# Attention's chunks 4 to 15 in 64x64 tiles on all array quarters, with the sign bit of the weights taken by 16-bit words

## The chip, the cores and the metric

The kernel runs on one core of one Trainium2 chip. The metric is the device time in microseconds of one execution.

## What is computed

A linear attention with decay, and two MLPs behind it. In short, from the reference:

```
gamma = 1.0 - 2.0 ** (-5.0 - arange(H))
for t in range(S):
    state = gamma * state + einsum('bhd,bhe->bhde', k[:, :, t], v[:, :, t])
    y[:, :, t] = einsum('bhd,bhde->bhe', q[:, :, t], state) / sqrt(D)
x = y as (tokens, heads * D)
h = x @ moe_w_in;   x = (h * sigmoid(1.702 * h)) @ moe_w_out
h = x @ moe2_w_in;  out = (max(h, 0) + alpha * min(h, 0)) @ moe2_w_out
```

There are 4 sequences of 768 tokens, 8 heads of 64 features (512 features in all), and 2048 hidden features in each MLP. The weights come as 64-bit floats, and the kernel turns them into 32-bit ones itself.

## The kernel before

**Attention in chunks.** The 3072 tokens are 24 chunks of 128, six to a sequence (`CPB`). A chunk has two stages. `att_scores` scales the values by the decay (eight instructions on ScalarE, ACT, line 326), multiplies keys by queries for each of the eight heads (line 333, tiles of 64 rows by 128 columns, two heads side by side on the two row halves of the array), and masks the result on VectorE (DVE, line 344, two instructions). `att_out` then makes, all on line 361: the update of the state from keys and values (128 rows by 64 columns), the output for the later 64 queries from all 128 keys (128 by 64), the output from the state of the chunks before (`diag`, 64 by 64, 128 queries moving) and the output of the first 64 queries from the first 64 keys (64 by 64). The heads are laid out so that the last two use all four quarters of the array. For that the keys and values of every second head are turned by 64 tokens on the host. The outputs lie in two PSUM tiles named px and pu; px also holds the update. `att_state` adds the update to `diag` and decays it (lines 398 and 401), `att_x` scales the outputs (line 413 or 431) and `att_x_low` splits off the low part (line 440). All attention products are plain fp32.

**MLPs.** Tokens go in six blocks of 512. The first layer on blocks 0 and 1 is done plainly: `mlp_h` makes 12 matmuls of 128x128 by 512 for a block and a piece of 128 hidden features, `mlp_y` 12 more. For the other blocks and the second layer pairs of blocks go through a seven-product scheme (`h_unit`, `y_chunk`, six matmuls a unit). High and low parts of each number are multiplied apart.

**Order of the work.** A table of slots says what is issued when: each step of `mlp_h` has two slots, and `job(slot, fn, ...)` puts attention stages and weight conversions there. Chunks 0 to 3 come before the first step, chunks 4 to 7 at slots 0 to 7, chunks 8 to 15 from slot `ATT1` = 36, chunks 16 to 23 with the first units of the seven-product scheme. The framework's scheduler may still move instructions between engines' queues by priority; each engine then runs its queue in order.

**Loads.** Queries and keys (`qk`) and keys and values (`kv`) of a chunk and the weights share a ring of five buffers (`issue`, `done`, `RING`); chunks 1 to 3 and 16 to 23 are loaded into free slots instead (`load_early`). Slots are 82 tiles of 128x512 words, taken and given back in turn (`take`, `give`).

**Weights.** `conv_words` reads the two 32-bit words of each 64-bit float on ACT (lines 183 and 184), `conv_f32` makes the 32-bit float on DVE: a minimum (190), a shift (193), an addition (196), and the sign bit, which one instruction with two tensors takes from the upper word and joins (197). It runs 64 times on 128x512.

## Time and profile before

| what | us |
|---|---|
| median of 3 runs (1042.81 to 1044.78) | 1042.84 |
| the profiled execution, its own time | 1043.22 |
| its span in the trace | 1041.4 |
| TensorE (PE) busy | 1024.5 |
| VectorE (DVE) busy | 890.1 |
| ScalarE (ACT) busy | 671.8 |

The span is the time from the first to the last instruction; the 1.8 us between it and the execution's time lie around it. PE is the matrix engine's matmul side; its weight loads are counted apart and overlap. Busy times of different engines overlap, so they don't add up. In the chain of waits the profile goes back from the last instruction to what released each one. The trace gives a record for each of two passes of an fp32 product, so eight products show as x16; the MLP's matmuls are one record each.

### The profile page before, as it was taken

The page shows a single profiled execution, that of the slowest core. Times are in us where ns is not written, and L with a number is a line of the kernel's source. Part 1 is how long each engine was busy: PE and PEld are TensorE (multiplying, and loading weights), DVE is VectorE, ACT ScalarE, POOL GpSimd, SP SyncE. Part 2 cuts the span into 40 slices and gives each one's busy share as a digit, 9 for nine tenths or more (in the row PEclk, how much of TensorE's full clock was granted, in tenths as well). Part 3 has the DMA queues.
Part 4 walks back from the last instruction along what each step waited for, and adds up shares of the span by engine and source line. Part 5 has one row for each costly group of instructions (what it writes and reads, how often), then busy time and mean ns, then how long its engine had stood idle before and what let it go on. Part 6 is the DMA issues. An engine that isn't in the chain of part 4 may idle for free.

```text
span 1041.4 us, 17905 instructions
## 1 busy us (share of the span) xinstructions
PE 1024.5 (98%) x5932; PEld 838.9 (81%) x5932; DVE 890.1 (85%) x1738; ACT 671.8 (65%) x1404; POOL 0.2 (0%) x4
## 2 busy tenths in 40 slices
PE   7999999999999999999999999999999999999998
PEld 5788887787778888888888887878888888888886
DVE  6999945998899999998899999999677978577792
ACT  6777746456676785665786777775555855556740
POOL 0000000000000000000000000000000000000000
PEclk9999999999999999999999999999999999999999
DMA  8679968689999889989989999896687666775671
GB/s 300 224 231 373 353 222 299 220 303 320 389 387 402 291 273 361 343 305 371 321 310 334 311 319 330 284 309 187 228 271 224 208 220 187 229 251 173 190 203 60
DMA packets 145532, 289.44 MB, mean 278 GB/s; under 512 B 16288, under 2 KB 16672, under 8 KB 145440
## 3 DMA queue, kind: packets, MB, share of 16 engines
q1 hardware_dynamic: 145152, 288.04, 80.6%
q8 instruction: 47, 0.77, 0.3%
q14 instruction: 45, 0.37, 0.1%
q10 hardware_dynamic: 288, 0.27, 0.1%
HBM read 213.79 MB, written 74.45 MB: 277 GB/s over the span
## 4 chain that ended last, share of the span: by engine, by line
PE 86%; DVE 7%; DMA 4%; ACT 1%; SPq 1%; issue 1%; DVEq 0%; ACTq 0%
PE py L705 36%; PE pa L632 20%; PE pd L632 15%; PE ph L530 6%; PE py L549 6%; PE px L361 2%; PE sc L333 1%; DMA hw<-wcin 1%; DVE wb L218 1%; DMA wo<-wo 1%; DVE s L260 1%; DVE a L344 1%; DMA ld<-kv 1%; DVE xo L458 1%; DMA early<-qk 1%
## 5 line engine op out<-in xcount | busy, mean ns | idle before, releaser
L705 PE MATMUL py<-gh,yw 128*128 128x512 f32 x1120 | 299.7, 389 | 0.9 <-ACT gw L644 0.7
L705 PEld LDWEIGHTS py<-gh,yw 128*128 128x128 f32 x1120 | 210.1, 188 | 45.2 <-ACT gw L644 1.1
L632 PE MATMUL pa<-xo,hw 128*128 128x512 f32 x912 | 231.5, 390 | 1.7 <-ACT gw L505 0.9
L632 PEld LDWEIGHTS pa<-xo,hw 128*128 128x128 f32 x912 | 170.7, 188 | 38.3 <-ACT gw L505 1.3
L514 DVE TENSOR_TENSOR gl<-gw,gh 128x512 fp32r<-128x512 f32 x240 | 160.9, 686 | 40.9 <-ACT gh L513 37.0
L513 ACT CAST gh<-gw 128x512 fp32r<-128x512 f32 x240 | 145.4, 620 | 56.7 <-PE py L705 25.0
L632 PE MATMUL pd<-xo,hw 128*128 128x512 f32 x684 | 173.2, 389 | 0.0
L705 PE MATMUL py<-gl,yw 128*128 128x512 f32 x560 | 172.7, 389 | 0.0
L632 PEld LDWEIGHTS pd<-xo,hw 128*128 128x128 f32 x684 | 128.2, 188 | 26.8
L705 PEld LDWEIGHTS py<-gl,yw 128*128 128x128 f32 x560 | 105.0, 188 | 22.1 <-DVE gl L514 0.4
L719 DVE TENSOR_TENSOR yc<-py,yc 128x512 f32<-128x512 f32 x99 | 63.7, 683 | 25.5 <-PE py L705 25.4
L506 DVE SCALAR_TENSOR_TENSOR gw<-t,nalpha,gw 128x512 f32<-128x512 f32 x96 | 71.2, 747 | 14.6 <-ACT gw L505 14.5
L504 ACT ACTIVATE t<-gw 128x512 f32<-128x512 f32 x72 | 45.4, 632 | 49.9 <-DVE gw L647 49.8
L214 ACT CAST wb<-s 128x256 fp32r<-128x256 f32 x128 | 47.4, 404 | 31.3 <-DVE s L260 18.7
L530 PE MATMUL ph<-xhi,wb 128*128 128x512 f32 x256 | 65.4, 396 | 1.3 <-ACT xhi L418 1.1
L549 PE MATMUL py<-gh,wb 128*128 128x512 f32 x256 | 65.5, 396 | 0.1
L644 ACT COPY gw<-pa 128x512 f32<-128x512 f32 x80 | 46.6, 585 | 24.6 <-PE pa L632 22.9
L530 PEld LDWEIGHTS ph<-xhi,wb 128*128 128x128 f32 x256 | 47.0, 188 | 12.0 <-ACT xhi L418 1.3
L549 PEld LDWEIGHTS py<-gh,wb 128*128 128x128 f32 x256 | 47.1, 188 | 11.6 <-ACT gh L513 0.6
L218 DVE TENSOR_TENSOR wb<-s,wb 128x256 fp32r<-128x256 f32 x128 | 49.7, 418 | 7.6 <-ACT wb L214 7.1
L647 DVE TENSOR_TENSOR gw<-pd,gw 128x512 f32<-128x512 f32 x80 | 54.8, 685 | 0.6 <-PE pd L632 0.5
L183 ACT ACTIVATE cvt<-ld 128x512 f32<-128x512 f32 x64 | 43.1, 673 | 17.2 <-DMA ld<-w 12.0
(93 smaller groups left out, 1373.3 us busy)
## 6 DMA issues: line engine op xcount, KB each, us to landing
hw<-wcin SPq DMA_DIRECT2D x266, 256.0 KB, 4.8
yw<-wcout SPq DMA_DIRECT2D x232, 256.0 KB, 3.7
ld<-w SPq DMA_DIRECT2D x64, 512.0 KB, 5.4
wcin<-wb SPq DMA_DIRECT2D x112, 256.0 KB, 5.3
wcout<-wb SPq DMA_DIRECT2D x88, 256.0 KB, 4.8
yw<-wo SPq DMA_DIRECT2D x48, 256.0 KB, 5.4
wo<-wb SPq DMA_DIRECT2D x32, 256.0 KB, 5.9
ld<-qk SPq DMA_DIRECT2D x13, 512.0 KB, 5.6
```

Of the source, the lines that this page charges most:

```text
L214: nc.scalar.copy(out=w[:, 0:256], in_=src)
L218: nc.vector.tensor_tensor(out=w[:, 256:], in0=src, in1=w[:, 0:256].bitcast(F32), op=ALU.subtract)
L506: nc.vector.scalar_tensor_tensor(out=g, in0=t, scalar=nalpha[:, ft:ft + 1], in1=g, op0=ALU.mult, op1=ALU.add)
L513: nc.scalar.copy(out=gh, in_=g)
L514: nc.vector.tensor_tensor(out=gl, in0=g, in1=gh.bitcast(F32), op=ALU.subtract)
L530: nc.tensor.matmul(out=ph, lhsT=cols(w, low, k), rhs=x[:, k, :], start=(n == 0), stop=(n == len(prods) - 1),)
L549: nc.tensor.matmul(out=py[e], lhsT=lhsT, rhs=g, start=(begin and seen[e] == 1), stop=(end and seen[e] == 3))
L632: nc.tensor.matmul(out=ps, lhsT=w[:, 256 * part_ + k * P:256 * part_ + (k + 1) * P], rhs=x[2 * k + low], start=(n in (0, 1, 3) and m == 0) ...
L644: nc.scalar.copy(out=chain[quad, n], in_=ps)
L647: nc.vector.tensor_tensor(out=g, in0=ps, in1=g, op=ALU.add)
L705: nc.tensor.matmul(out=ps[e], lhsT=w[:, at:at + P], rhs=t, start=(fresh and seen[e] == 1), stop=(m == GQ - 1 and seen[e] == 3), skip_group ...
L719: add_ = lambda o, x: nc.vector.tensor_tensor(out=o, in0=ps, in1=x, op=ALU.add)
```

## The change

Chunks 0 to 3 and 16 to 23 (`WHOLE`) are done whole: `whole_scores` as before, and `whole_out` with the state products on two quarters (row half s to column half 1 - s) and one product of all 128 keys by all 128 queries for each head. The turned layout of keys and values goes.

Chunks 4 to 15 are done as two halves (`sub` 0 and 1) of 64 tokens. One `att_step(o, new)` makes the output of chunk `o` and the scores and updates of chunk `new`, all as 64x64 products with 64 columns moving, and `att_products` lays them out alternately: the output from row half s goes to column half 1 - s (px), scores and updates from row half s to column half s (sc, pu). Between the halves stands a middle state, `mid`. The update gives it and the next `diag`, of which there are now two. `att_v` is a stage of its own, one slot ahead. Chunks 4 to 7, 14 and 15 are loaded into slots, chunks 8 to 13 by the ring.

In the conversion, the low three bits go into the lower 16-bit half of a word on ACT; the sign is put into the upper half by an AND on 16-bit words of one tensor on DVE, and the addition joins both.

```diff
-        nc.scalar.activation(out=r, in_=w0.bitcast(U32), func=AF.Copy, scale=2.0**-29)
+        low = r.bitcast(U16).rearrange("p (n t) -> p n t", t=2)[:, :, 0]
+        nc.scalar.activation(out=low, in_=w0.bitcast(U32), func=AF.Copy, scale=2.0**-29)
...
+        nc.vector.tensor_scalar(
+            out=r.bitcast(U16).rearrange("p (n t) -> p n t", t=2)[:, :, 1], in0=top, scalar1=0x8000, scalar2=None,
+            op0=ALU.bitwise_and,
+        )
         nc.vector.tensor_tensor(out=ti, in0=ti, in1=r, op=ALU.add)
-        nc.vector.scalar_tensor_tensor(
-            out=ti, in0=w1.bitcast(I32), scalar=-2**31, in1=ti, op0=ALU.bitwise_and, op1=ALU.bitwise_or
-        )
...
+    def whole_out(c):
...
+        heads = [(p, s, slice(p * C, (p + 1) * C), 2 * p + s) for p in range(NP) for s in range(2)]
+        for p, s, _, h in () if last else heads:
+            product(pu, s, slice(p * D, (p + 1) * D), kt[:, h * D:(h + 1) * D], v[:, h, :])
+        if not first:
+            for p, s, at, h in heads:
+                product(px, 1 - s, at, diag[c % 2][ROWS[s], p, :], qt[ROWS[s], at])
+        for p, s, at, h in heads:
+            product(px, 1 - s, at, v[:, h, :], a[s][:, p, :])
...
+        def from_state(c, sub, p, s):
+            src = att["mid", c] if sub else None if c % CPB == 0 else diag[c % 2]
+            if src is not None:
+                qt = loaded["qk", c][0]
+                product(att["px", c], 1 - s, block(2 * p + sub), src[rows[s], p, :], qt[rows[s], block(2 * p + sub)])
+
+        def from_chunk(c, sub, p, s):
+            n = NP * sub + p
+            product(att["px", c], 1 - s, block(2 * p + sub), att["v", c][rows[s], n, :], att["a", c][rows[s], n, :])
+
+        def score(c, sub, p, s):
+            qt, kt = loaded["qk", c]
+            at = block(2 * p + sub)
+            product(att["sc", c], s, block(NP * sub + p), kt[rows[s], at], qt[rows[s], at])
+
+        def update(c, sub, p, s):
+            if sub == 0 or c % CPB != CPB - 1:
+                n = NP * sub + p
+                kt = loaded["kv", c][0]
+                product(att["pu", c], s, block(n), kt[rows[s], block(n)], att["v", c][rows[s], n, :])
+
+        each = [(sub, p) for sub in range(2) for p in range(NP)]
+        old = []
+        if o is not None:
+            lo, hi = each[:NP], each[NP:]
+            turn_ = [(from_state, lo), (from_chunk, lo), (from_chunk, hi), (from_state, hi)]
+            old = [(f, o, *at) for f, ats in turn_ for at in ats]
+        fill = [(f, new, *at) for f in (score, update) for at in each] if new is not None else []
+        turns = [t for pair in zip(old, fill) for t in pair] if old and fill else old + fill
+        for at in range(0, len(turns), 2):
+            for n, s in ((0, 0), (1, 1), (0, 1), (1, 0)):
+                turns[at + n][0](*turns[at + n][1:], s)
...
+    def att_state(c):
+        pu = att.pop(("pu", c)).rearrange("p (m n d) -> p m n d", m=2, d=D)
+        mid = att["mid", c] = take("mid", (P, NP, D))
+        if c % CPB == 0:
+            nc.scalar.copy(out=mid, in_=pu[:, 0])
+        else:
+            nc.vector.tensor_tensor(out=mid, in0=pu[:, 0], in1=diag[c % 2], op=ALU.add)
+        if c % CPB != CPB - 1:
+            new = diag[(c + 1) % 2]
+            dec = decay_c.unsqueeze(2).to_broadcast([P, NP, D])
+            nc.vector.tensor_tensor(out=new, in0=pu[:, 1], in1=mid, op=ALU.add)
+            nc.vector.tensor_tensor(out=new, in0=new, in1=dec, op=ALU.mult)
...
+        if c < 2 * per:
+            s, gap = 2 * (c - per), 1 + (c < 2 * per - 1)
+            job(s + gap + 1, att_x_low, c)
         else:
-            s = base + c - 4 * per
-        attention(c, s, s + 1, s + 1, s + 2)
+            s, gap = ATT1 + 2 * (c - 2 * per), 2
+        turn_at.setdefault(s, {})["new"] = c
+        turn_at.setdefault(s + gap, {})["o"] = c
+        if c in RINGED:
+            job(s - LEADS[c // per][1], att_v, c, load=(("qk", c), ("kv", c)))
+        else:
+            job(s - LEADS[c // per][0], load_early, c)
+            job(s - LEADS[c // per][1], att_v, c)
+    for s, t in turn_at.items():
+        job(s, att_step, t.get("o"), t.get("new"))
```

What moves on PE, at chunk 8: sc is the tile of scores, py an output of the first MLP, a the masked scores, v the scaled values. Before, from the last scores to the output stage:

```order
L333 MATMUL sc_1851<-ld 128x128
L333 MATMUL sc_1852<-ld 128x128
L549 MATMUL py_1089<-gh,wb 128x512 x2
L549 MATMUL py_1090<-gh,wb 128x512 x2
L549 MATMUL py_1091<-gh,wb 128x512 x2
L549 MATMUL py_1092<-gh,wb 128x512 x2
L549 MATMUL py_1089<-gl,wb 128x512
L549 MATMUL py_1090<-gl,wb 128x512
L549 MATMUL py_1091<-gl,wb 128x512
L549 MATMUL py_1092<-gl,wb 128x512
L361 MATMUL px<-v,ld 64x64 x8
L361 MATMUL px<-a_1861,v 64x64
```

Now, between two groups of the MLP (ph is its hidden part), the first products of the step that ends one chunk and begins the next:

```order
L628 MATMUL py_1157<-gl,wb 128x512
L609 MATMUL ph<-xhi,wb 128x512 x8
L609 MATMUL ph<-xlo,wb 128x512 x4
L406 MATMUL px<-ld,diag_82 64x64
L406 MATMUL sc<-ld 64x64
L406 MATMUL px<-ld,diag_82 64x64
```

So 12 MLP matmuls no longer stand between scores and output of a chunk, and outputs of one chunk alternate with scores of the next; 24 MLP matmuls stand between two steps.

What moves on ACT, at the first MLP step: v is the scaled values of chunk 4, g the first gate, gh its rounding, wb pieces of weights, x the outputs of chunk 3. Before:

```order
L214 CAST wb<-cvt 128x256 x2
L418 CAST xhi<-x_457 128x4x128
L326 ACTIVATE v<-ld,cst 128x64 x8
L183 ACTIVATE cvt<-ld 128x512
L184 ACTIVATE cvr<-ld 128x512
L501 ACTIVATE g<-ph 128x512
L513 CAST gh<-g 128x512
L214 CAST wb<-cvt 128x256 x2
```

Now:

```order
L499 CAST xhi<-x_439 128x4x128
L183 ACTIVATE cvt<-ld 128x512
L216 CAST wb<-cvt 128x256 x2
L185 ACTIVATE cvr<-ld 128x512
L580 ACTIVATE g<-ph 128x512
L396 ACTIVATE v<-early,cst 128x64
L592 CAST gh<-g 128x512
L396 ACTIVATE v<-early,cst 128x64 x7
L216 CAST wb<-cvt 128x256 x4
```

The eight value instructions of chunk 4 stood before the gate; now one stands behind the gate and seven behind the rounding.

What moves on DVE around the mask of chunk 4 (a); xlo is the low part of chunk 3's outputs, cvt and cvr are a weight in conversion, wb its pieces. Before:

```order
L398 TENSOR_TENSOR t<-px,diag 128x256
L218 TENSOR_TENSOR wb<-cvt,wb 128x256
L401 TENSOR_TENSOR diag<-t,cst 128x256
L344 TENSOR_TENSOR a_535<-sc_525,cst 128x512
L344 TENSOR_TENSOR a_537<-sc_526,cst 128x512
L440 TENSOR_TENSOR xlo<-x_457,xhi 128x4x128
L218 TENSOR_TENSOR wb<-cvt,wb 128x256
```

Now:

```order
L519 TENSOR_TENSOR xlo<-x_439,xhi 128x4x128
L194 TENSOR_SCALAR cvt<-cvt 128x512
L220 TENSOR_TENSOR wb<-cvt,wb 128x256 x2
L197 TENSOR_SCALAR cvr<-ld 128x512
L191 TENSOR_SCALAR cvt<-cvt 128x512
L201 ISA cvt<-cvt,cvr 128x1024
L194 TENSOR_SCALAR cvt<-cvt 128x512
L197 TENSOR_SCALAR cvr<-ld 128x512
L191 TENSOR_SCALAR cvt<-cvt 128x512
L468 TENSOR_TENSOR a<-sc,cst 128x512
```

The mask of chunk 4 stood ahead of the low part of chunk 3; now it stands behind it and behind nine conversion instructions, and is one instruction in place of two. The sign bit (cvr from ld) has become an instruction of its own.

## Rows read from the trace of the kernel before

**Rows 1.** The page: span, busy time of each engine, the chain's shares.
```profile
span 1041.4 us, 17905 instructions
...
PE 1024.5 (98%) x5932; PEld 838.9 (81%) x5932; DVE 890.1 (85%) x1738; ACT 671.8 (65%) x1404; POOL 0.2 (0%) x4
...
PE 86%; DVE 7%; DMA 4%; ACT 1%; SPq 1%; issue 1%; DVEq 0%; ACTq 0%
```
**Rows 2.** Timeline of PE, 60 to 74 us: start, length, line, tiles, form, count.
```profile
63.13 1.98 PE L549 MATMUL py<-gh,wb 128*128 128x512 f32 x8
...
65.85 1.98 PE L530 MATMUL ph<-xhi,wb 128*128 128x512 f32 x8
```
**Rows 3.** Timeline of PE, 139 to 147 us: one chunk's two stages.
```profile
139.66 1.16 PE L333 MATMUL sc<-ld 64*128 64x128 f32 x16
140.76 2.11 PE L549 MATMUL py<-gh,wb 128*128 128x512 f32 x8
...
143.71 0.69 PE L361 MATMUL px<-v,ld 128*64 128x64 f32 x16
...
144.28 0.22 PE L361 MATMUL px<-a,v 128*64 128x64 f32 x1
...
144.63 0.22 PE L361 MATMUL pu<-a,v 128*64 128x64 f32 x1
...
144.95 0.28 PE L361 MATMUL px<-ld,diag 64*64 64x128 f32 x2
...
145.06 0.28 PE L361 MATMUL px<-ld,diag 64*64 64x128 f32 x2
...
145.28 0.22 PE L361 MATMUL px<-a,v 64*64 64x64 f32 x2
145.29 0.22 PE L361 MATMUL pu<-a,v 64*64 64x64 f32 x2
...
145.45 0.23 PE L361 MATMUL px<-a,v 64*64 64x64 f32 x2
...
145.62 1.43 PE L530 MATMUL ph<-xhi,wb 128*128 128x512 f32 x5
```
**Rows 4.** Busy time by stretch: length, PE, PEld, DVE, ACT, POOL, clock, DMA.
```profile
0.00:20.00 20.00, 15.63 (x246) 11.24 (x248) 11.25 (x26) 12.56 (x38) 0.20 (x4) 1.00 0.94 346
...
23.57:60.50 36.93, 34.01 (x380) 26.41 (x374) 34.42 (x78) 28.58 (x76) 0.00 (x0) 1.00 0.59 203
139.66:209.66 70.00, 68.50 (x790) 54.53 (x790) 49.78 (x131) 34.06 (x98) 0.00 (x0) 1.00 0.71 243
251.93:316.64 64.71, 63.51 (x762) 51.82 (x762) 56.12 (x141) 43.51 (x114) 0.00 (x0) 1.00 1.04 389
330.00:645.00 315.00, 315.00 (x1392) 260.91 (x1391) 298.59 (x569) 222.04 (x437) 0.00 (x0) 1.00 0.93 326
```
**Rows 5.** Timeline of PE, 175 to 183 us: output stage of chunk 12, first records.
```profile
179.68 0.69 PE L361 MATMUL px<-v,ld 128*64 128x64 f32 x16 [0.73 <-DVE a L344]
```
**Rows 6.** Who waited for whom, 23.57 to 60.5 us: total, times, longest.
```profile
PE sc L333 <- DMA ld<-qk: 1.6, 1, 1.6
...
PE ph L530 <- ACT xhi L418: 1.1, 1, 1.1
```
**Rows 7.** Timeline of ACT, 24 to 31 us: values of chunk 4, first gate.
```profile
25.67 2.02 ACT L326 ACTIVATE v<-ld,cst 128x64 f32<-128x64 f32 x8
...
29.58 0.60 ACT L501 ACTIVATE g<-ph 128x512 f32<-128x512 f32 x1 [0.24 <-PE ph L530]
```
**Rows 8.** Groups of DVE by line and form: busy, mean ns, idle before.
```profile
L197 DVE SCALAR_TENSOR_TENSOR cvt<-ld,cvt 128x512 int32<-128x512 int32 x64 | 43.6, 686 | 0.2
...
L193 DVE TENSOR_SCALAR cvt<-cvt 128x512 int32<-128x512 int32 x64 | 26.6, 422 | 0.4
```
**Rows 9.** Timeline of PE, 644 to 699 us: two rows with a wait.
```profile
646.75 1.66 PE L632 MATMUL pa<-xo,hw 128*128 128x512 f32 x6 [0.92 <-ACT gw L505]
...
695.95 1.17 PE L705 MATMUL py<-gh,yw 128*128 128x512 f32 x4 [0.68 <-ACT gw L644]
```

More of the change, by code (lines that the diff above doesn't have):

```diff
@@ L46 @@
 NQ = NF // 2
+WHOLE = [c for c in range(NCH) if not BT // C <= c < 4 * BT // C]
 X_OF = ("b11", "b21", "t2", "t1", "t3", "b22", "t4")
@@ L102, in tile_linear_attention_two_mlps @@
     nalpha = cpool.tile([P, NF], F32, name="nalpha")
-    diag = cpool.tile([P, NP, D], F32, name="diag")
+    diag = [cpool.tile([P, NP, D], F32, name=f"diag{i}") for i in range(2)]
     part = dram.tile([2, P, 2, BT], F32, name="part")
@@ L353, in att_out, with product @@
         kt = loaded.pop(("kv", c))[0]
-        px = [att_psum(c, which, [P, 512]) for which in ("px", "pu")]
-        pu = px[0][:, 2 * C:].rearrange("p (n d) -> p n d", n=NP)
+        px, pu = att_psum(c, "px"), None if last else att_psum(c, "pu")
         fresh = set()
-        def product(bank, half, cols, lhsT, rhs):
-            begin = (bank, half) not in fresh
-            fresh.add((bank, half))
+        def product(ps, half, cols, lhsT, rhs):
+            begin = (id(ps), half) not in fresh
+            fresh.add((id(ps), half))
@@ L361, in product @@
             nc.tensor.matmul(
-                out=px[bank][half * D:(half + 1) * D, cols], lhsT=lhsT, rhs=rhs,
-                start=begin, stop=True, skip_group_check=True,
-            )
-        heads = [(p, s, p % 2, s ^ p % 2, p // 2 * C) for p in range(NP) for s in range(2)]
-        if not last:
-            for p, s, _, _, _ in heads:
-                cols = slice((2 * p + s) * D, (2 * p + s + 1) * D)
-                product(0, s, slice(2 * C + p * D, 2 * C + (p + 1) * D), kt[:, cols], v[:, 2 * p + s, :])
@@ L371, in att_out @@
[L371 to L379 removed]
+                out=ps[ROWS[half], cols], lhsT=lhsT, rhs=rhs, start=begin, stop=True, skip_group_check=True,
+            )
@@ L385, in att_out @@
             done()
-        att[c] = px, None if last else pu
-        if c != BT // C - 1:
-            with tc.high_priority(HG):
-                att_state(c)
-    def att_state(c):
-        first = c % CPB == 0
-        att[c], pu = att[c]
-        if pu is not None:
-            src = pu
-            if not first:
-                src = take("t", (P, NP, D))
-                nc.vector.tensor_tensor(out=src, in0=pu, in1=diag, op=ALU.add)
-                give(src)
+        att["px", c] = px
@@ new lines, in whole_out, with att_v @@
+        with tc.high_priority(HG):
+            if not last:
+                src, new = pu[:, :NP * D].rearrange("p (n d) -> p n d", n=NP), diag[(c + 1) % 2]
+                if not first:
+                    nc.vector.tensor_tensor(out=new, in0=src, in1=diag[c % 2], op=ALU.add)
+                    src = new
+                dec = decay_c.unsqueeze(2).to_broadcast([P, NP, D])
+                nc.vector.tensor_tensor(out=new, in0=src, in1=dec, op=ALU.mult)
+            att_x(c)
+    def att_v(c):
+        v = take("v", (P, 2 * NP, D))
+        dec = decay_v[C if c in WHOLE else HC]
+        vt = loaded["kv", c][1].rearrange("p (n d) -> p n d", d=D)
+        for n in range(2 * NP):
+            nc.scalar.activation(out=v[:, n, :], in_=vt[:, n, :], func=AF.Copy, scale=dec[:, n:n + 1])
+        att["v", c] = v
@@ new lines, in att_products, with product, block @@
+    def att_products(o, new):
+        rows = [slice(s * D, (s + 1) * D) for s in range(2)]
+        fresh = set()
+        def product(ps, half, cols, lhsT, rhs):
+            begin = (id(ps), half) not in fresh
+            fresh.add((id(ps), half))
+            nc.tensor.matmul(
+                out=ps[rows[half], cols], lhsT=lhsT, rhs=rhs, start=begin, stop=True, skip_group_check=True,
+            )
+        def block(n):
+            return slice(n * D, (n + 1) * D)
+        def from_state(c, sub, p, s):
[26 more added lines that the diff above has]
+                turns[at + n][0](*turns[at + n][1:], s)
@@ L845, in tile_linear_attention_two_mlps @@
                     add(key, src_of(key))
[L847 removed]
+    rank = [conv_hi, att_x_low, whole_out, whole_scores, att_step, att_v]
     def run(slot):
```

228 lines of the change are left out of this document (112 added, 116 removed), and 6 rows, old and new, of tables (AT_WHOLE, EARLY).

## The prediction

> **What bounds the kernel now.** I read the page first. TensorE (PE) is busy 1024.5 of 1041.4 us, and PE is 86% of the chain that ended last [rows 1]. So a change pays here only where it shortens the time that PE's own stream takes, or removes one of PE's few waits. VectorE (DVE) with 890.1 us busy is the next engine; it matters in the two places where it runs full.
>
> PE's stream consists of MLP matmuls and attention. The timeline of a stretch without attention gives the MLP's pace: a group of 12 matmuls follows the one before after 65.85 - 63.13 = 2.72 us, so 0.2267 us each [rows 2]. Then I read one ordinary chunk, start to start [rows 3]. Its 8 score products (16 records: each fp32 product is recorded twice) take from 139.66 to 140.76, 1.10 us. The 12 MLP matmuls behind them take 2.95 in place of 2.72, so 0.23 for getting back to the full array. Its output stage of 64 records takes from 143.71 to 145.62, 1.91 us, and the way back costs 0.22 again. **A chunk costs 1.10 + 0.23 + 1.91 + 0.22 = 3.46 us of PE.**
>
> Inside, the same rows show the pace by tile form:
> - 128 rows by 64 columns, 64 moving columns: a pair of records every 58 ns (six pairs from 144.28 to 144.63); both column halves work.
> - 64x64 tiles, 128 moving columns: four records every 110 ns (144.95, 145.06), all quarters busy.
> - 64x64 tiles, 64 moving columns: 145.28 and 145.29 hold four records, one on each quarter, and the rounds follow to 145.45, 0.17 / 3 = 57 ns; I use 58, as for the other form of 64 columns.
>
> So the score stage is 8 rounds of two at 110 ns, 0.88 us, and 0.22 of entry and exit. The output stage is 0.47 (state update, 128x64) + 0.47 (later half, 128x64) + 0.44 (from the state, quarters) + 0.23 (first half, quarters) = 1.61, and 0.30 of entry, exit and one change of tile form, which therefore costs about 0.1.
>
> **Chunks 8 to 15.** Before, the stretch is 70.00 us [rows 4]; it holds 15 groups of 12 MLP matmuls, 180 x 0.2267 = 40.8, so attention costs 29.2. By the pattern it would be six chunks at 3.46 and two without update or state (output 1.44) at 2.99, together 26.7; the other 2.5 are waits, such as those of 0.73 us for the masked scores [rows 5].
> After, a joint step does the output of one chunk and the scores and update of the next: 64 products of 64x64x64, 128 records. If all quarters run, that is 32 rounds x 58 ns = 1.86; with 0.22 entry and exit and 0.22 for the MLP behind it, 2.30. There are nine steps: seven joint ones, one that only begins and one that only ends. The two single ones have 64 records but use two quarters, so they take the same 32 rounds; steps at a sequence's edge do too, since the fuller quarters have 32. 9 x 2.30 = 20.7. The gain is 8.5 if the waits go as well, 6.0 if all stay. What a step reads (masked scores, scaled values, middle state) is now made a whole step before, 24 MLP matmuls or 5.4 us, instead of 12; so most waits should go. **I take -7.5, ends -8.5 and -6.0.**
>
> **Chunks 4 to 7.** From the scores of chunk 4 to the end of chunk 7: 36.93 us [rows 4], 84 MLP matmuls in it (19.0), so 17.9 for attention and waits; two of the waits are 1.6 us for a load of q and k and 1.1 for the first x [rows 6]. After: five steps x 1.86, six entries with their way back (the order cuts the first steps apart) x 0.44, and about 0.7 for products that run on two quarters there: 12.6. PE's own demand falls by 5.3. The load's wait should go, since chunks 4 to 7 now load into slots and no longer share the ring of five with weights. But DVE is busy 34.42 of those 36.93 us [rows 4], so not all of it can be had. And ACT's order shows **a new wait**: the scaled values of chunk 4 stood ahead of the first gate and ended at 27.7 [rows 7]; now one of the eight is behind the gate and seven behind the cast after it. The update of chunk 4 needs all eight; PE stands in order behind it with chunk 4's output, and the second MLP step behind that. The first MLP products last 2.8 us and end at about 28.7; then 0.60 for the gate, 0.25 for a value, as much as the gate for the cast, 1.75 for seven values (by 2.02 / 8) [rows 7]: 31.9. PE has 1.4 us of scores and state products until then, 30.1. That is up to 1.8 us, less what still overlaps: 1.5. The mask of chunk 4, which PE needs too, has nine more conversion instructions ahead of it on DVE. **I take -2.0, ends -5 and +2.**
>
> **Chunks 0 to 3** become whole again, and their output stage gets dearer (next paragraph): 3 x 0.7. But PE waits there for loads and for the values from ACT: it is busy 15.63 of the first 20 us [rows 4]; the extra matmuls fall into these waits, and state products no longer need the mask. If the cover were gone, 2.1. **I take 0, ends -1 and +2.1.**
>
> **Chunks 16 to 23** are whole too, in a stretch where PE is busy 63.51 of 64.71 us [rows 4]: nothing hides it. State products use two quarters in place of four: 8 rounds of 110 ns for 4, +0.44. The masked part takes all 128 keys for 128 queries: 16 records of 128x64 with 128 moving columns. The trace has none of that form; twice the 58 ns of 64 columns or the 110 ns of the 64-row form bound it, 0.88 to 0.93, against 0.47 + 0.23: +0.18. One change of form more: +0.1. That is 0.72 for five chunks, 0.62 for the two that end a sequence (no update, no extra change of form), 0.1 for chunk 18 that begins one: 3.6 + 1.2 + 0.1. **I take +4.9, ends +3.9** (a wait at chunk 18 gone) **and +5.5.**
>
> **The sign bit.** 64 times, a three-operand step of 0.686 us on DVE becomes a single-source AND on 16-bit words. The nearest rows are the shift of the same 512 elements, 0.422, and the old step [rows 8]; I take 0.42, since it too has one source, and 0.69 is the other end. That frees 64 x 0.26 = 17 us of DVE. The masks of chunks 4 to 15 become one instruction in place of two, against one more addition each. On PE's path most of it is worth nothing: from 330 to 645 us PE has no gap at all. Right behind it PE waited 0.92 and 0.68 us for ACT, and some more [rows 9], with DVE full while the second layer's weights are converted; part of that can go. **-0.6, ends -2.0 and +0.5** (slots are reused in another order). The extra copies of the middle state, and att_v's earlier place, are on ACT, which has room there.
> The Trainium skill (VectorE: DVE Perf Modes, "What auto-detection actually checks") gives a one-source operation in SBUF two elements per cycle; no row here shows it for strided 16-bit words.
>
> **Sum:** -7.5 - 2.0 + 0 + 4.9 - 0.6 = -5.2. The profiled execution took 1043.22 us (span 1041.4), so 1038.0; the median of the runs shown is 0.4 lower, so **1037.6**.
>
> **Rivals.**
> *Twice the gain at the start* (0.13): DVE and the ring, not PE, set the pace from 24 to 46 us, and 4 to 5 us go there, with all waits of chunks 8 to 15: -8.5 - 4.5 + 4.9 - 1.5 = -9.6, 1033.2. For it: DVE 93% busy there; against: the new wait on ACT.
> *No difference* (0.13): the first stage is bound by loads and ACT, so chunks 4 to 7 bring nothing, chunks 0 to 3 pay 1.5, and the waits of chunks 8 to 15 only move: -6.0 + 0 + 1.5 + 4.9 = +0.4, 1043.2.
> *Slower, because four quarters are not kept busy for long* (0.06): the trace shows a round of four in 58 ns for four rounds in a row only. A joint step needs 32, with eight PE instructions (four weight loads, four matmuls) each. If PE can be fed only as fast as in the 128-column rounds, eight per 110 ns, each of 14 steps takes 32 x 52 ns = 1.66 us more: +23, 1061. The change stops paying when a round takes 58 + 5200 / 448 = 70 ns.
> *Half rate by the bank* (0.02): the two row halves write one PSUM bank (the two records of px), and would take turns: a round is 116 ns, +26 us, 1063.5. Against it: in [rows 3] px x2 at 145.28 are the two row halves in one bank, and pu's pair begins 0.01 later. The Trainium skill (TensorEngine Tiling (Array Packing), "Gotcha 1: PSUM Pressure") says that different row tiles cannot access one bank at the same time; the trace, where they write different partitions of it, does not agree.
>
> **How the numbers follow.** My forecast has 0.66. Its own range, from the ends of the terms taken together as independent, is about 4 either way. The range of 1032.5 to 1042.5 takes in the first rival and half of the second. A measurement tells 0.2% (2.1 us) from no change: faster means under 1040.8. Forecast 0.66, of which 0.06 lies above that; first rival 0.13: faster 0.73. The 0.06 and most of the second rival make no difference: 0.16. The rest of it, the third and the fourth: 0.11.
>
> **What would show it.** In the timeline a joint step of chunks 8 to 15 should hold 128 records in 2.1 us, rounds of four 58 ns apart; over 70 ns the forecast is wrong. The stretch of these chunks should shrink by 7.5. Chunks 16 to 23 should show 2.6 us of output stage. The AND should show 0.42 us. ACT's values of chunk 4 should stand behind the first gate, with PE waiting for them near 30 us. If PE's gaps before 60 us grow by more than 3 us, or the stretch from 645 to 700 gets longer, the sum fails there.

## The result, and the profile after

The changed kernel takes 1050.28 us (median of 11 runs, 1046.53 to 1053.61), the kernel before 1043.32 us on the same chip (11 runs, 1042.33 to 1046.73). The ratio is 1.006, 95% interval 1.0044 to 1.0077: **slower** by 0.6%, outside of the range that was predicted. The profiled execution of the changed kernel took 1048.7 us, its span is 1046.8; it is one of the quicker of the 11, so its loss of 5.4 us against the span before is less than the 7.0 of the medians.

The page of the changed kernel:
```profile
span 1046.8 us, 18649 instructions
...
PE 1027.5 (98%) x6316; PEld 844.8 (81%) x6316; DVE 872.4 (83%) x1730; ACT 678.1 (65%) x1406; POOL 0.2 (0%) x4
```
Beside [rows 1] VectorE has 17.7 us less to do, ScalarE 6.3 more, and TensorE is busy for longer. To see where the 5.4 us of the spans came from, I noted in both timelines of PE when each stage begins:

| PE reaches | before | after | behind by |
|---|---|---|---|
| the first MLP matmul | 25.82 | 26.81 | 1.0 |
| the 348 MLP matmuls behind chunk 7 | 60.28 | 65.30 | 5.0 |
| chunk 8's scores | 139.66 | 144.54 | 4.9 |
| chunk 16's scores | 251.93 | 254.63 | 2.7 |
| the MLP behind chunk 23 | 316.42 | 322.14 | 5.7 |
| the end of the last matmul | 1037.60 | 1040.82 | 3.2 |
| the end of the span | 1041.4 | 1046.8 | 5.4 |

(The last step is not the change's: the stretch behind the last matmul, whose code is the same, is 3.8 us before and 6.0 here; in the other runs below, with the same code, it is 3.8 to 3.9, 4.9 or 5.9.)

The tiles did what was computed. Timeline of PE, the first joint step's first record (chunk 8's output with chunk 9's scores), its last and the MLP behind it:
```profile
152.22 0.27 PE L406 MATMUL px<-ld,diag 64*64 64x64 f32 x1
...
154.10 0.22 PE L406 MATMUL pu<-v,ld 64*64 64x64 f32 x1
154.24 0.50 PE L628 MATMUL py<-gh,wb 128*128 128x512 f32 x1
```
154.24 - 152.22 = 2.02 us for 128 records (2.08 was computed); six of the seven joint steps of chunks 8 to 15 stand in the timeline with 2.02 to 2.35, one with 4.10. An output stage of a whole chunk, same view:
```profile
260.03 0.69 PE L362 MATMUL pu<-v,early 128*64 128x64 f32 x16
260.64 1.09 PE L362 MATMUL px<-early,diag 64*64 64x128 f32 x16
261.66 1.09 PE L362 MATMUL px<-a,v 128*64 128x128 f32 x16
```
The next record stands at 262.69: 2.66 in place of 1.91, so +0.75 where +0.72 was computed.

The loss is in waits and in what follows them. Busy time by stretch, columns as in [rows 4]:
```profile
26.81:65.30 38.49, 34.97 (x565) 28.61 (x565) 35.90 (x85) 34.45 (x88) 0.00 (x0) 0.91 0.64 214
28.00:32.00 4.00, 4.00 (x31) 2.78 (x31) 3.27 (x9) 1.48 (x4) 0.00 (x0) 0.57 0.94 357
62.00:66.00 4.00, 4.00 (x67) 3.79 (x67) 3.52 (x10) 2.32 (x6) 0.00 (x0) 0.57 0.31 58
204.00:208.00 4.00, 3.31 (x13) 2.61 (x13) 4.00 (x12) 2.23 (x5) 0.00 (x0) 0.50 0.72 265
144.54:214.56 70.02, 67.05 (x1186) 55.63 (x1185) 50.17 (x139) 35.20 (x101) 0.00 (x0) 0.95 0.80 286
254.63:322.14 67.51, 67.51 (x633) 54.64 (x632) 54.90 (x139) 45.00 (x114) 0.00 (x0) 1.00 0.97 359
```
Who waited for whom in the changed kernel, 20 to 66 us and 182 to 216 us (total, times, longest):
```profile
PE px L406 <- DVE x L495: 3.5, 1, 3.5
PE ph L609 <- ACT xhi L499: 1.8, 1, 1.8
...
PE px L406 <- DVE diag L486: 2.1, 2, 1.9
PE pu L406 <- issue: 0.8, 1, 0.8
```
Three waits, of 1.8 us ahead of the first MLP matmul, 3.5 ahead of chunk 7's output and 1.9 ahead of the last joint step (chunk 14's output with chunk 15's scores), are each followed by a stretch whose granted clock is at the lower level, 1.2 GHz (0.5; two of the rows show 0.57, since they reach beyond it). There the first 12 MLP matmuls took 4.41 us in place of 2.95, chunk 7's output 3.42 in place of 2.01, the 24 MLP matmuls behind the last joint step 7.44 in place of 5.67. In the profiled execution before, the clock was 1.00 in every stretch [rows 4].

A fourth wait stands among the 168 MLP matmuls that follow chunk 15, with no low clock behind it (timeline of PE):
```profile
246.24 2.11 PE L628 MATMUL py<-gh,wb 128*128 128x512 f32 x8 [1.47 <-ACT gh L592]
```
All twelve kernels here and below that do chunks 8 to 15 in halves have one at this place, of 1.5 to 3.8 us; the four with attention as before have none over 0.8. In this run ScalarE, which makes gh, had stood 3.26 us for VectorE's sums just ahead of it; what lies behind that stays open.

### The profile page after: what moved, and what is told of

It is laid out like the page before. It is cut to its first block, busy times and chain, and to the rows that moved or that the text cites. A ratio compares the mean times of both kernels' runs of the same rounds, so it can differ in the third digit from the quotient of the medians.

```text
span 1046.8 us, 18649 instructions
## 1 busy us (share of the span) xinstructions
PE 1027.5 (98%) x6316; PEld 844.8 (81%) x6316; DVE 872.4 (83%) x1730; ACT 678.1 (65%) x1406; POOL 0.2 (0%) x4
## 4 chain that ended last, share of the span: by engine, by line
PE 86%; DVE 5%; DMA 4%; ACT 3%; SPq 1%; issue 0%; DVEq 0%; ACTq 0%
PE py L784 36%; PE pa L711 21%; PE pd L711 16%; PE ph L609 5%; PE py L628 4%; PE px L362 2%; DMA ld<-kv 1%; ACT v L396 1%; DMA wcin<-wb 1%; DVE wb L220 1%; PE sc L340 1%; DVE s L262 1%; PE pu L362 1%; DMA early<-kv 1%; DMA early<-qk 1%; PE px L406 0%
## 5 line engine op out<-in xcount | busy, mean ns | idle before, releaser
L747 DVE TENSOR_TENSOR gw<-gw 128x512 f32<-128x512 f32 x80 | 53.5, 686 | 0.4
```

Of the source, the lines that this page charges most:

```text
L747: sub = lambda o, x, y: nc.vector.tensor_tensor(out=o, in0=x, in1=y, op=ALU.subtract)
```

## Experiments

**Theory "waits"** at the start: the tiles' gain went into TensorE's waits for VectorE's queue, and each is made dearer by the low clock behind it. **Rivals:** the 64x64 work itself lowers the clock; the sign bit does it, by slots or by ScalarE; late fetches of TensorE's instructions. Later ones: transfers set the pace of chunks 8 to 15; order, or amount of work, at the start. Intervals below are of the ratio to the kernel before.

### The sign bit alone, and attention alone

The kernel before with only `conv_words` and `conv_f32` of the change (`sign_only`), and the changed kernel with these two as before (`old_sign`).

> The kernel before with the sign bit by 16-bit words alone, no change of attention. Theory 'waits' gives this part the 2.5 us that the changed kernel gained behind 322 us (no stalls near 646 and 696 any more): 2 to 2.5 us faster than before, 1041. Rival 'slots' (that gain comes from another order of slots or loads, and the conversion on ScalarE to every second 16-bit word, 0.78 in place of 0.67 us, gives back what VectorE saves): within 0.5 us of before.

> The change with the sign bit taken as before (a three-operand step of 0.69 us on VectorE), attention as in the changed kernel: the part on attention alone. Theory: the two parts add up. The sign bit alone gave 3.5 us less on the kernel before, so without it the changed kernel should be slower by 2.5 to 4 us, 1053 to 1054, most of it behind 322 us and ahead of 65 us, and attention alone costs 10 us against the kernel before. Rival 'slots': the 16-bit step has no part in it, 1050 as the changed kernel.

`sign_only`: 1039.86 us, ratio 0.9971 (0.9959 to 0.9983), **faster** by 0.3%. No wait of PE behind 315 us is left ([rows 9] are two of those before), the 348 matmuls begin at 58.11 in place of 60.28. `old_sign`: 1047.26, ratio 1.0038 (1.0024 to 1.0051), where 1053 to 1054 was expected. So attention alone costs 0.4%, and the parts don't add up: in the changed kernel the sign bit saves 2.3 us behind 322 us (PE waits 2.15 us at 675 without it) but the 348 matmuls begin at 65.30 with it and 61.03 without. Of these 4.3 us 2.9 are low clock (1.46 and 1.41), which the profiled execution of `old_sign`, the quickest of its twelve at 1043.68, did not have; so only the other 1.4 can be laid to the sign bit. Against `sign_only`, which differs in attention alone, the changed kernel is 7.2 us behind there. The groups of the changed kernel (ns min/median/max), of DVE and ACT:
```profile
L197 DVE TENSOR_SCALAR cvr<-ld x64: 448/466/485, 15.0 to 655.4; 128x512 uint16<-128x512 uint16 x64
...
L185 ACT ACTIVATE cvr<-ld x64: 759/787/807, 12.4 to 632.1; 128x512 uint16<-128x512 uint32 x64
```
The step that VectorE lost cost 0.686 [rows 8], the new one 0.466. But ScalarE's half now writes every second 16-bit word, and takes 0.787 where before it took 0.672. That is 64 x 0.115 = 7.4 us, of which the first stage has a sixth.

### The start: chunks 0 to 7

`halves8` keeps chunks 4 to 7 whole, in the slots of before:
```diff
-WHOLE = [c for c in range(NCH) if not BT // C <= c < 4 * BT // C]
+WHOLE = [c for c in range(NCH) if not 2 * BT // C <= c < 4 * BT // C]
```
`x_first` takes x out of PSUM first (for chunk 3, and in each joint step):
```diff
         with tc.high_priority(HG):
+            if o is not None:
+                att_x(o)
             if new is not None:
...
-            if o is not None:
-                att_x(o)
```

> The change with only chunks 8 to 15 in halves; chunks 4 to 7 stay whole, in the slots that they had before the change. Theory 'waits': what the change lost ahead of 65 us came with chunks 4 to 7; with them whole the block of 348 MLP matmuls begins at about 62 (60.28 before the change, plus 4 x 0.4 for the dearer whole form; 65.30 with the change), without a stretch at half clock ahead of it, and the time falls by about 3.3 us to 1047. Rival 'the loss is in chunks 0 to 3' (whole form, late x of chunk 3, loads): the first MLP matmul still comes at 26.8 and the slow stretch behind it stays; the block begins at 64 or later, and the time falls by 1 us or less.

> The change with the outputs x taken out of PSUM first on VectorE: chunk 3's before the update of the state, and in a joint step the old chunk's before the mask and the middle state of the new one. Theory 'waits' (the gain of the 64x64 tiles went into new waits of TensorE for VectorE's queue, and the granted clock falls to a half after each of them): the wait of 1.8 us for the first x_hi gets about 0.7 shorter, the one of 3.45 us ahead of chunk 7's output falls to about 1.2; both slow stretches behind them (28 to 31.4, 62.4 to 65.6) go, the first MLP group takes 2.95 in place of 4.41, chunk 7's output 2.1 in place of 3.42, the block of 348 MLP matmuls begins near 60 in place of 65.3, and the time falls by 4 to 5 us to about 1045.5. Rival 'clock by the tiles' (the 64x64 work itself brings the clock down, or the chip does so for another reason): the waits may shorten, the slow stretches stay; at most 2 us.

`halves8`: 1047.59, ratio 1.0049 (1.0031 to 1.0066). The 348 matmuls begin at 62.93, with the clock at 1.00 from 28 to 68 us. In `x_first`, `spread` and `sums_apart`, which have halves there and kept the clock up at 28 us too, they begin at 62.87, 63.43 and 63.71. So in chunks 4 to 7 the halves gained nothing against whole chunks in their new form. `x_first`: 1047.95, ratio 1.0046 (1.0029 to 1.0064). The first wait fell from 1.8 to 1.5 and the slow clock behind it did not come, but it did not come in `spread` and `sums_apart` either, behind 1.8 us; the one ahead of chunk 7's output stayed at 3.1, with the slow clock behind it. So x's place was not the cause of the longer wait, and only 0.4 us of the first.

Then I took work off one engine: `no_clamp` leaves the minimum of the first ten weight blocks out, `pool_v` gives the scaled values of chunks 4 to 7 to GpSimd.

> The change without the clamp (a minimum, 0.42 us on VectorE) of the first ten weight blocks of the first layer: that part of the computation is left out, 10 x 0.34 = 3.4 us of VectorE's queue between 24 and 60 us. Theory 'VectorE sets the pace at the start': the wait of 3.3 us ahead of chunk 7's output shrinks by most of this, to 1 us or less, the clock does not fall behind it, the block of 348 MLP matmuls begins at 61 to 62 (65.3 in the changed kernel, of which 1.7 was the slow clock at 28 us; 62.9 to 63.7 in the runs without that), and the time falls by 3 us or more. Rival 'ScalarE sets it' (24 of 24 us busy from 32 to 56, against 17.8 before the change): VectorE only waits more for ScalarE's halves of the conversion, the wait stays over 2.5 us.

> The change with the scaled values of chunks 4 to 7 made by GpSimd, which has nothing else to do, in place of ScalarE: 32 instructions of 0.25 us, 8 us of ScalarE between 24 and 60 us. Theory 'ScalarE sets the pace at the start': the wait of 3.3 us ahead of chunk 7's output goes or falls under 1 us, and the one for the scaled values at 30 us too; the block of 348 MLP matmuls begins at 61 or earlier, the time falls by 3 us or more. Rival 'VectorE sets it': the wait falls by less than 1 us. If GpSimd needs over 0.6 us for each of the 64-column products, or holds up VectorE, the values themselves come late and the wait grows.

`no_clamp`: 1050.17, ratio 1.0066 (1.0045 to 1.0086); `pool_v`: 1050.65, ratio 1.0064 (1.0043 to 1.0085). Both missed. In `pool_v` GpSimd took some 0.88 us for each instruction, over the 0.6 that the expectation named, yet chunk 7's values were ready at 49.9 us, ahead of 51.6 in the changed kernel, so they were not what came late. The wait ahead of chunk 7's output (waits of PE, 20 to 66 us, `no_clamp`):
```profile
PE px L407 <- DVE x L496: 4.8, 1, 4.8
```
and `pool_v`:
```profile
PE px L411 <- DVE x L500: 3.9, 1, 3.9
```
VectorE's own order suggests why less work did not help: in `no_clamp` 11 converted blocks stand ahead of chunk 7's mask, in the changed kernel 10. The freed time seems to have gone to conversions that nobody waits for yet. `held` therefore keeps the conversions behind attention's instructions of their slot:
```diff
-            convert((kind, 1, ft), m - 2 * per + CS if ft < LEAD else ...
+            convert((kind, 1, ft), m - 2 * per + CS + 2 * n if ft < LEAD else ...
...
-        nc.vector.tensor_tensor(out=ti, in0=ti, in1=r, op=ALU.add)
+        pin(nc.vector.tensor_tensor(out=ti, in0=ti, in1=r, op=ALU.add))
```
(`pin` is `tc.keep_in_program_order` in slots 1 to 9; it stands around all conversions but the casts to fp32r.) `held_less` is `held` without that minimum.

> The change with VectorE's and ScalarE's conversions of the first ten weight blocks held behind attention's instructions of their slot (they may no longer be put ahead of them), and the five output blocks among them converted two slots later. In VectorE's order the mask of chunk 7 moves from place 107 to 93, with 8 converted blocks ahead of it in place of 10. Less work for VectorE (no clamp) or for ScalarE (values on GpSimd) changed nothing, because freed time was filled with conversions that come later. Theory 'order' (what TensorE waits for ahead of chunk 7's output is the place of chunk 7's mask, middle state and x of chunk 6 in VectorE's queue, not how much work there is): 14 operations x 0.34 = 4.8 us earlier; the wait of 3.3 us falls under 1 us, no slow clock behind it, the block of 348 MLP matmuls begins near 60.5 (63.4 to 63.7 in runs without the slow clock at 28 us), the time falls by 3 to 5 us to 1046. Rival 'work': the weights are then late, TensorE waits for them between 28 and 62 us or right behind, and the block begins at 63 or later.

> The run 'held' without the clamp of the first ten weight blocks (that part of the computation is left out). In 'held' the wait ahead of chunk 7's output is gone, and TensorE waits 3.7 us for late weight blocks in its place; with less work but the old order ('no_clamp') the freed time went to conversions that come later. Theory 'work in the right order' (VectorE has more to do up to 62 us than fits, in whatever order): with the order held, 10 x 0.34 = 3.4 us less work now shows: the waits for weight blocks fall from 3.7 to 1 us or less, the block of 348 MLP matmuls begins at 61.5 or earlier where the clock stays up at 28 us (64.55 in 'held', of which 1.6 was slow clock). Rival 'latency' (the weights are late because of ScalarE or because each step waits in turn for the other engine): the waits stay over 2.5 us.

`held`: 1048.81, ratio 1.0049 (1.0034 to 1.0064). Waits of PE, 20 to 66 us:
```profile
PE ph L615 <- DVE wb L226: 3.7, 3, 2.1
PE ph L615 <- ACT xhi L505: 1.8, 1, 1.8
```
The wait for x is gone, and 3.7 us of waits for weight blocks stand in its place; the 348 matmuls begin at 64.55 (1.6 of it from a slow clock at 28 us). In the changed kernel chunk 7's scores end at 54.55 us and its mask begins 4.3 us later, behind 105 operations of VectorE. Here it has 91 ahead of it and begins 0.3 us behind its scores; but these end at 58.73, since TensorE had waited for weights, so the mask comes no earlier (59.01 us for 58.85). `held_less` (1051.57, ratio 1.0075, 1.0052 to 1.0097) still waits 3.2 us for them: there VectorE stood 1.8 us for ScalarE's cast of g and 1.5 for the middle state that ScalarE copies for chunk 6, and ScalarE 1.6 for a weight's load. So at the start a wait that is removed comes back at another place; it runs through VectorE, ScalarE and loads in turn. Which one would have to be shortened first stays open, and no run took work off both engines. What is shown is that neither 3.4 us of VectorE nor 8 us of ScalarE, nor the order of VectorE's queue, does it alone.

### Chunks 8 to 15

`sums_apart` moves two jobs of sums away from chunks 13 to 15, and two more by one or two slots. `spread` moves sums and stores of the first layer ahead of chunk 8:
```diff
-SUMS_IN = (37, 41, 45, 49, 53, 56, 59, 62)
+SUMS_IN = (29, 31, 33, 35, 53, 56, 59, 62)
-STORE_W = (24, 0.9)
+STORE_W = (20, 0.85)
```
`shift` puts 72 one-column matmuls behind the warming-up ones (and 8 of those in place of 12), to move where TensorE's instruction blocks end.

> The change with two jobs of VectorE and ScalarE moved away from chunks 13 to 15: the sums of the first layer's output weights 8 and 9 from slot 47 to 43, the sums of its input weights 6 and 7 from slot 49 to 53. Theory 'waits': chunk 14's masks no longer come 2 us late, the wait of 1.9 us at 199 to 201 us and the smaller one behind the step before go, with them the slow clock from 202.5 to 208.5; the last joint step takes 2.02 in place of 4.10, the two MLP groups around it 5.7 in place of 7.66 and 7.44; the time falls by about 5 us to 1045. A part of it may come back as a wait at slot 44 to 46. Rival 'instruction feed' (the hole of 1.2 us in the last joint step is a late fetch of TensorE's instructions, whatever VectorE does): the hole and the slow clock behind it stay, and only 2 us are gained.

> The change with work of the queues moved ahead of chunk 8: the sums of the first layer's input weights 0 to 7 from slots 37, 41, 45, 49 to 29, 31, 33, 35, and its stores 4 slots earlier (20 + 0.85 m in place of 24 + 0.9 m). In the changed kernel the transfers stand still from 128 to 144 us (share 0.11 and 0.00) and are full from 160 to 196 us (share 0.97 to 1.08), VectorE works 0.85 of 4 us at 176 to 180 and is behind by 2 us at 197. Theory 'transfers' (the joint steps shorten the stretch of chunks 8 to 15, but not what its transfers and VectorE have to do in it; they, not TensorE, set its pace): share under 0.9 at 160 to 196, no wait of over 0.7 us from 175 to 202, the first whole score at 251.5 in place of 254.6, the time lower by about 3 us, 1047. Rival 'instruction feed': the hole in the last joint step (1.2 us here, 1.6 to 1.9 us in two of the runs so far) stays, and with it half of the loss. Rival 'VectorE is full before too' (95% and more from 72 to 120 us): the moved sums make the weights late and TensorE waits from 90 to 140 us, nothing is gained.

> The change with 72 more one-column warming-up matmuls and 4 fewer long ones ahead of everything, so that some 136 more TensorE instructions lie ahead of attention; they run while TensorE waits for the first loads. Nothing else differs but a few rows of chunk 4. A fetch of 16 KB of TensorE's instructions takes 0.9 to 1.2 us and begins each time some 300 records are gone through; in all runs so far the one of the last joint step begins inside of it, and TensorE has a hole there with no wait. Theory 'instruction feed': the hole depends on where the fetch falls, so it goes from the last joint step, to another one or away; the step itself takes about 2.0 and a wait before it. Time lower by 1 to 2 us, or the same if another step has it. Rival 'the hole is a late wait or a transfer': it stays in the last joint step, at 0.8 to 1.9 us.

`sums_apart`: 1046.17, ratio 1.0031 (1.0016 to 1.0045). Waits of 1.15 and 1.38 us came at 182 to 185 and 1.6 remained at 201: the backlog only moved, as I had feared, though no slow clock came behind these waits. `spread`: 1045.25, ratio 1.0015 (1.0003 to 1.0027): three quarters of the loss gone. Busy time by stretch, changed kernel:
```profile
136.00:144.00 8.00, 8.00 (x37) 6.60 (x37) 2.51 (x6) 2.03 (x4) 0.00 (x0) 1.00 0.00 0
...
168.00:176.00 8.00, 8.00 (x173) 6.69 (x167) 3.71 (x9) 3.90 (x12) 0.00 (x0) 1.00 1.01 391
...
184.00:192.00 8.00, 7.76 (x149) 6.32 (x143) 7.87 (x21) 6.04 (x20) 0.00 (x0) 1.00 1.02 369
```
and `spread`:
```profile
168.00:176.00 8.00, 8.00 (x173) 6.69 (x165) 3.70 (x9) 2.29 (x7) 0.00 (x0) 1.00 0.68 187
...
184.00:192.00 8.00, 6.86 (x97) 5.52 (x93) 7.98 (x21) 7.21 (x21) 0.00 (x0) 1.00 0.74 287
```
The column before the last is the DMA share. In the changed kernel the transfers stand still just ahead of chunk 8 and are full from 160 to 196 us. SyncE, which issues loads and stores, stood from 126 to 147 us for chunk 8's step (waits of SP, 120 to 150 us, changed kernel and then `spread`; before it was 11.7):
```profile
SPq L151 <- PE pu L406: 20.5, 1, 20.5
...
SPq L151 <- PE pu L406: 5.6, 1, 5.6
```
Then the rest has 14% less time than before (7.69 us a chunk in place of 8.90), since that is what the tiles shorten. VectorE is not full at first, it waits for a transfer (timeline of DVE, changed kernel):
```profile
178.20 0.42 DVE L262 TENSOR_TENSOR s<-cvt 128x256 f32<-128x256 f32 x1 [4.68 <-DMA wcin<-wb]
```
From 184 to 192 us it works 7.87 of 8 us, and it comes 1.9 us late to the last joint step. The longest such wait before was 1.1 us, and `spread` has none. With the work moved, the wait ahead of the last joint step and the slow clock behind it are gone (one of 1.1 us ahead of the step before is left, and 1.9 at 241.90 for gh), and from chunk 8's scores to chunk 16's it takes 250.31 - 143.72 = 106.6 us; before 112.3, in the changed kernel 110.1. So the tiles give 5.7 us there once this work is out of the way, against 7.5 predicted and 2.2 seen. `spread` moved VectorE's sums and the stores together, so which of the two counts for more is not shown.

Of the rest, part goes with the rival "instruction feed". Timeline of PE, last joint step of the changed kernel:
```profile
201.01 0.29 PE L406 MATMUL px<-early,diag 64*64 64x64 f32 x2 [1.89 <-DVE diag L486]
...
203.53 0.31 PE L406 MATMUL px<-early,mid 64*64 64x64 f32 x1
204.69 0.26 PE L406 MATMUL pu<-v,early 64*64 64x64 f32 x1 [0.85 <-issue]
```
Nothing was waited for at 204.69. In the DMA view of 202.0 to 203.5 one fetch of instructions stands:
```profile
q8 instruction: 1, 0.02, 4.9%
```
It is a block of 16 KB, it began at 202.23 and took 1.18 us. In the other joint steps of this run such fetches began behind the step, in MLP matmuls. `shift` (1051.87, ratio 1.0062, 1.0043 to 1.008) moved them by about half a block, and the hole went to chunk 12's step (a fetch at 177.86); timeline of PE there:
```profile
180.36 0.27 PE L406 MATMUL pu<-v,ld 64*64 64x64 f32 x1 [0.82 <-issue]
```
In its last joint step there is no hole, though a fetch begins inside it, 1.4 us behind its start. The rival stands as a second cause: each of the twelve kernels with the halves has one such hole, of 0.45 to 1.86 us, in a step in which a fetch begins, and in all twelve TensorE goes on 1.3 to 1.5 us behind the end of that fetch. What it does between the two is not shown, and eight other fetches, which began 1.4 us or more behind the start of a step, left no hole. It does not explain the waits ahead of the step, which `shift` kept (2.0 us).

### The clock

`pauses` is the kernel before; behind five units, VectorE works through 2 to 9 operations before the next weights are let go:
```diff
+        for n in range(count):
+            nc.vector.tensor_scalar(out=t, in0=ps if n == 0 else t, scalar1=0.0, scalar2=None, op0=ALU.mult)
+        w = yw[0]
+        nc.vector.tensor_tensor(out=w[:, 0:512], in0=w.bitcast(F32), in1=t, op=ALU.add)
```

> The kernel before with five pauses of TensorE between 380 and 560 us, where it has no 64x64 products and no gap: TensorE waits there for a chain of 2, 3, 5, 7 and 9 operations of VectorE that begins when TensorE's last unit is done, about 1.5, 2, 2.8, 3.6 and 4.5 us long. Theory 'waits' (the granted clock falls after TensorE stood idle, whatever it did before): behind the pauses of 2 us and more the granted clock is 0.5 for about 3 us, and the MLP matmuls there take twice as long, some 1.5 us each time; behind the shorter one it stays 1.0. Rival 'clock by the tiles': it is 1.0 behind all five.

One run, 1083.42 us. VectorE had older work ahead of the chain, so the pauses became 9.1, 4.6, 7.2, 4.5 and 6.5 us long, and the short ones that I wanted are missing. Busy time by stretch, behind the first two:
```profile
587.00:592.00 5.00, 4.85 (x12) 3.82 (x13) 4.41 (x11) 1.21 (x2) 0.00 (x0) 0.50 0.97 333
592.00:596.00 4.00, 4.00 (x19) 3.32 (x18) 2.51 (x5) 2.24 (x4) 0.00 (x0) 0.99 0.82 297
...
635.00:639.50 4.50, 4.35 (x10) 3.47 (x11) 4.50 (x11) 1.24 (x2) 0.00 (x0) 0.50 0.90 289
640.00:644.00 4.00, 4.00 (x19) 3.29 (x18) 3.97 (x8) 1.80 (x3) 0.00 (x0) 1.00 0.51 164
```
Behind all five the clock was at 0.5 for 3 to 5 us, with no 64x64 product near: the rival "clock by the tiles" falls for pauses of this length. For the waits of 1.8 and 1.9 us this run shows nothing; the first of them, in the changed kernel, comes ahead of any product of the halves. Over whole executions the mean granted clock was 0.992 to 0.997 in the 11 runs of the changed kernel, and 0.995 to 1.000 in the 24 of the kernel before beside `sign_only`, so the kernel before can have a low stretch too.

### Both causes together, and the best version

`best_held` joins `held`, `spread` and chunk 3's x first; `sign_spread` is `sign_only` with the moves of `spread`, without the tiles.

> The same, with the sums and stores moved ahead of chunk 8 as in the run 'spread' and chunk 3's x ahead of its state. Theory 'order' and 'transfers' add up: the first whole score at 247 to 248 (254.6 in the changed kernel, 250.3 with the moves alone), 1041 to 1042, level with the kernel before or a little faster; still behind the sign bit and the moves without the tiles (1036.7), since the whole chunks cost 3.0 us behind 250 and about 2 ahead of 24. Rival 'work': 1045 as with the moves alone.

> The kernel before with the sign bit by 16-bit words and the same moves of sums and stores as in the run that moves them in the changed kernel. Theory 'transfers': the waits of chunks 8 to 15 there (1.08 us ahead of the scores or outputs at 175 to 181, 0.5 near 158, 0.2 each near 195 to 204: some 2.4 us) go in part, 1038; the rival 'VectorE is full before too' gives 1040 or more.

`best_held`: 1047.12, ratio 1.0032 (1.0019 to 1.0044), a miss: the 348 matmuls begin at 64.85. `sign_spread`: **1036.74 us** (1036.41 to 1037.35), ratio 0.9932 (0.992 to 0.9943), faster than both kernels. From 20 to 252 us its longest wait of PE is 1.2 us.

## Why the prediction was wrong

- *Chunks 8 to 15, -7.5 (seen -2.2).* The steps' own time was right (2.02 and 0.23 for the way back, 2.30 computed). The step that failed is "What a step reads ... is now made a whole step before ... so most waits should go": that looked at TensorE's distance alone. The stretch of before had a DMA share of 0.71 as a mean [rows 4], and I did not ask what of it lay where; it stood near idle as the stretch began and near full from 147 to 179 us. Two windows of the kernel before:
```profile
139.00:147.00 8.00, 8.00 (x102) 6.36 (x101) 4.02 (x11) 2.74 (x6) 0.00 (x0) 1.00 0.16 46
...
163.00:171.00 8.00, 8.00 (x84) 6.26 (x76) 5.00 (x13) 3.28 (x8) 0.00 (x0) 1.00 0.97 325
```
At full speed, nine steps of 2.02 with 0.23 each and 360 MLP matmuls of 0.2267 would take 101.9 us up to chunk 16's scores (an estimate); the changed kernel took 110.1. Of the 8.2 between, the wait ahead of the last joint step is 1.9, the low clock behind it 1.8, the excess of that step 2.1 and the wait at 246.24 1.5. `spread` brought the term to -5.7.
- *Chunks 4 to 7, -2.0 (seen +4.0).* "PE's own demand falls by 5.3" was no measure where PE is not the bound. I had the row (DVE busy 34.42 of 36.93 us) and kept a gain all the same. The new wait that I named, for chunk 4's values (1.5), came in pieces too short for the list of waits. Timeline of ACT:
```profile
32.57 1.78 ACT L396 ACTIVATE v<-early,cst 128x64 f32<-128x64 f32 x7
```
TensorE's last 50 records ahead of 34.78 follow these values from 32.97 on, 1.8 us where rounds of 58 ns would take 0.7. The one for chunk 7's output, 3.5, I did not see; chunk 7 alone has one slot, not two, between its scores and its output, which may be why it falls there. The sign bit, with ScalarE's dearer half, put 7 operations more ahead of chunk 7's mask than `old_sign` has, where the mask begins 3.0 us behind its scores in place of 4.3.
- *Chunks 0 to 3, 0 (seen +1.0).* The step that failed is "the extra matmuls fall into these waits": chunk 3's output ended at 25.02 us in place of 23.64, so VectorE began its x at 25.42 in place of 24.36, and the first MLP matmul waits 1.8 in place of 1.1 [rows 6]. That x now comes behind the state is 0.4 of the 1.0: `x_first` has the matmul at 26.44.
- *Chunks 16 to 23, +4.9 (seen +3.0).* The price of a whole chunk was right (0.75 for 0.72). But chunk 18's output and the scores behind it, forecast at +0.1, came out 1.0 shorter (1.49 and 1.09 us in place of 2.31 and 1.31), the lower end of the term, and 0.9 us went too between chunk 22's scores and its output, where TensorE had waited 0.7 for a load; that I had not priced.
- *Sign bit, -0.6 (seen -2.5 behind 322 us).* Too small, and the operation dearer than taken (0.466 for 0.42). That ScalarE pays for it was not in the sum.
- *Not in the sum at all:* the low clock behind waits (4.6 us by the three stretches named above) and the instruction fetch inside a step. No row of the kernel before showed either.
- *The rivals.* "Four quarters not kept busy" as I priced it fell (58 ns held for 32 rounds), but its idea, that instructions can't come fast enough, fits the hole in one step per run. "Half rate by the bank" fell: the Trainium skill (TensorEngine Tiling (Array Packing), "Gotcha 1: PSUM Pressure") says that different row tiles cannot access one bank at the same time; the 2.02 us do not agree, since rounds of 116 ns would make a step some 3.9. The right forecast, new waits where PE stops being the bound, stood among the rivals only as "waits ... only move", at +0.4; the measured +7.0 lies far outside of that too.

## What to carry to other kernels

Where a change shortens the bounding engine's own stream, list for that stretch what transfers and the other engines must still do in it, and look at them in windows of a few us, not by the mean: they can become the bound, and a stretch that stands idle just ahead of it is room to move work into. Price a wait on TensorE at its length plus, where it is long, the low clock behind it (1.4 to 1.8 us in the changed kernel). And try the parts apart: here one part alone, with the sums and stores moved, gave 0.7%, and no run with the other was faster than the kernel before.

## What the runs showed of the hardware

- **The clock behind idle time.** In the sixteen profiled executions, behind 20 us and ahead of the last matmul, 17 of 19 idle times of TensorE of 3.0 us or more were followed by a stretch at 0.5, and 9 of 40 between 1.4 and 3.0 us; no such stretch came without one of these. So the same wait of 1.8 us ahead of the first MLP matmul cost 1.8 us in `spread` and 3.3 in the changed kernel. The runs of the changed kernel spread by 7 us and those of `sign_spread` by 1, but those of the kernel before spread by 4.4, so that the clock makes the spread is not shown. The Trainium skill (TensorE: Matmul & The Clock Gate, "What's actually happening") names the same two levels, 1.2 and 2.4 GHz, for an array that was idle or busy. The clock records of these runs agree: they hold 0.5 and 1.0 alone.
- **Instruction fetch.** The Trainium skill (Runtime: NRT & Kernel Launch, "Instruction fetch mechanics") calls the crossing of a 16 KiB block mostly hidden. In MLP matmuls these runs agree: 24 of them with such a fetch among them took 5.67 us, 24 x 0.2267 and the 0.23 of the way back. But a joint step of 2.02 us with 256 records of matmuls and weight loads shows, where a fetch begins inside it, a hole of up to 1.9 us, though not each time.
- **Writing every second 16-bit word.** ScalarE's conversion of 512 elements took 0.787 us so, and 0.672 to whole words.
